# Attention scores for all heads at once on the two row halves, with a new start order, in a fused attention and MLP kernel

## The chip, the cores and the metric

One core of one Trainium2 chip runs the kernel. The metric is the device time in microseconds (us) of one execution. A kernel's time here is the median of four or seven executions; none of them was in the slow state (over 1.5% above the fastest of its kernel). The profile is one execution, whose span (first to last instruction) is about 2 us shorter than its time. In profiles TensorE, which does the matmuls, is PE (its weight loads are PEld), VectorE is DVE, ScalarE is ACT, and GpSimd is POOL, which also issues most of the loads (DMA). TensorE writes its results to PSUM, a memory that the kernel uses in eight banks.

## The reference, cut to what matters

Four batches, 8 heads, 768 positions, head width 64. Each query sees the 96 keys up to itself and the first 8 keys of the batch, with a bias that falls with distance. The result, rearranged to 3072 tokens of 512 numbers, goes through an MLP with a squared relu.

```python
keep = is_global | is_local            # 8 global keys, 96 local keys
scores = scale * q @ k.T + bias        # bias = -slope[h] * dist
a = exp(where(keep, scores, -1e9)); a /= a.sum()
x = (a @ v) rearranged to (3072, 512)
h = x @ w_in                           # 512 x 2048
out = (relu(h) ** 2) @ w_out           # 2048 x 512
```

Work goes by 24 tiles of 128 positions, 6 to a batch. As keys reach back at most 95 positions, a tile needs its own keys and those of the tile before (a batch's first tile only its own). The MLP goes by 12 blocks of two tiles, with w_in and w_out each cut into 8 pieces.

## The kernel before

The program is a list of operations with costs. A small planner in the kernel file orders them when the program is built; that order is then fixed on each engine. `load` names when a late tile's data is expected, and `any_copy` is a copy on either VectorE or ScalarE.

Scores: two heads share the 128 rows. To get the two heads' scores apart with one full-height matmul, q is padded: the rhs holds head 0 over zeros beside zeros over head 1.

```python
for pair in range(0, NPAIR, per):               # one PSUM bank for a head pair
    sc = ps_sc.tile([P, 2, 2, P], FP32)         # 2 banks, used in turn
    for i in range(2):                          # own keys, keys of the tile before
        nc.tensor.matmul(out=sc[:, i, :, :], lhsT=kT[kj][:, p_, :],
                         rhs=qz[zi][:, p_, :, :])    # 256 columns, half of them zeros
    # exp on ScalarE, times exp(bias) on VectorE, then at x v
```

Softmax sums come from a column of ones that stands beside v. It is set first of all:

```python
nc.vector.memset(zero.bitcast(I32), 0)
for j in range(NT):                                    # all 24 tiles
    nc.vector.memset(v_sb[j][:, :, D : D + 1], 1.0)    # the ones columns
make_identity(nc, ident)                               # on POOL
load_qk(1)
# ... masks on POOL ...
load_v(0); load_v(1)
# ... then T2 i0 T3 o0 i1 o1 i2 o2 i3 o3 T4 i4 o4 i5 o5 T5 i6 o6 i7 o7
#     (T: q, k, v of a tile; i, o: a piece of w_in, w_out)
...
ld = plan.op(("load", j), {"POOLQ": 2.6}, emit_load, ..., ready=clock[0])  # tiles 6 to 23
```

The softmax here doesn't subtract the row's maximum and nothing guards it: scores larger than these inputs give would overflow.

## Time and profile before

| | before |
|---|---|
| time | 225.8 us (225.67 to 226.42) |
| TensorE busy | 211.1 us, 94% of a span of 223.7 |
| TensorE's waits from 30 us on | 0.7 us |
| first MLP matmul | 19.38 us |

The lines are in the prediction below. Busy time is the union of records; what an instruction really takes from the next one is read from start to start.

### The profile page before, as it was taken

Reading aid. Unit: us, or ns where it says so; the run is one execution under the profiler, and the core shown is the slowest. Engines: PE = TensorE matmul, PEld = TensorE weight load, DVE = VectorE, ACT = ScalarE, POOL = GpSimd, SP = SyncE. Lnnn points to the kernel's source line nnn. Section 1 sums busy time; section 2 is a strip of 40 time slices with the busy share of each in tenths; the row PEclk is TensorE's granted clock in tenths of the full one; section 3 lists DMA queues with packets and bytes.
Section 4 is the critical chain, followed back from the end, with each engine's and each line's share of the span. In section 5 each row is a group of like instructions: output and inputs, shape, how many; then the busy total and the mean of one; then the engine's idle time right before and its main releaser. Section 6 shows DMA issues by size and latency. Waiting matters only on the chain.

```text
span 223.7 us, 4803 instructions
## 1 busy us (share of the span) xinstructions
PE 211.1 (94%) x1817; PEld 151.9 (68%) x1848; DVE 146.1 (65%) x380; ACT 123.3 (55%) x225; POOL 88.0 (39%) x118
## 2 busy tenths in 40 slices
PE   6499999999999999999999999999999999999992
PEld 2388677765777777766767777776776676676750
DVE  6466857677766868757666866866756856844530
ACT  3359666674755944645644745734645644643530
POOL 8996677799978985505605000000000000000000
PEclk9979999999999999999999999999999999999998
DMA  9999999999999999998999984256524430300202
GB/s 132 102 148 199 183 197 180 175 174 169 167 146 151 152 171 169 134 214 98 163 166 129 124 118 95 67 124 95 143 54 90 131 70 13 117 11 17 94 0 94
DMA packets 115142, 27.83 MB, mean 124 GB/s; under 512 B 105776, under 2 KB 112176, under 8 KB 115120
## 3 DMA queue, kind: packets, MB, share of 16 engines
q0 software_dynamic: 79424, 13.38, 79.5%
q1 hardware_dynamic: 35696, 14.16, 32.6%
q8 instruction: 14, 0.23, 0.4%
q14 instruction: 8, 0.07, 0.1%
HBM read 27.26 MB, written 6.29 MB: 150 GB/s over the span
## 4 chain that ended last, share of the span: by engine, by line
PE 82%; POOL 6%; DVE 4%; DMA 4%; ACT 2%; issue 1%; POOLq 0%
PE acc L723 35%; PE hT L659 35%; PE sc L442 7%; PE po L549 4%; DMA win<-in_moe_w_in_dram 4%; DVE hs L692 2%; POOL v L186 1%; POOL q L186 1%; POOL k L186 1%; ACT hr L680 1%; DVE o L299 1%; POOL win L186 1%; PE trx L611 1%; POOL wout L186 1%; ACT qz L297 1%
## 5 line engine op out<-in xcount | busy, mean ns | idle before, releaser
L659 PE MATMUL hT<-xT,win 128*128 128x256 bf16 x768 | 98.6, 273 | 0.5 <-ACT xT L297 0.4
L680 ACT ACTIVATE hr<-hT 128x512 f32<-128x512 f32 x96 | 57.3, 597 | 74.7 <-PE hT L659 72.7
L723 PE MATMUL acc<-wout,hs 128*128 128x512 bf16 x353 | 94.8, 379 | 1.6
L659 PEld LDWEIGHTS <-win 128*128 128x128 bf16 x768 | 74.7, 98 | 23.4 <-DMA win<-in_moe_w_in_dram 0.7
L692 DVE TENSOR_TENSOR hs<-hr 128x512 bf16<-128x512 f32 x96 | 65.9, 687 | 25.7 <-ACT hr L680 24.3
L723 PEld LDWEIGHTS <-hs 128*128 128x128 bf16 x384 | 34.5, 98 | 22.8
L482 ACT ACTIVATE esc<-sc 128x512 bf16<-128x512 f32 x78 | 46.2, 593 | 2.4 <-PE sc L442 2.3
L442 PE MATMUL sc<-qz,kT 128*128 128x256 bf16 x176 | 35.3, 276 | 0.7 <-ACT at L482 0.4
L503 DVE TENSOR_TENSOR at<-esc,E 128x512 bf16<-128x512 bf16 x78 | 32.4, 417 | 0.1
L186 POOL DMA_DIRECT2D qpad<-in_q_dram x28 | 21.6, 800 | 23.0 <-DMA qz<-qpad 23.0
L186 POOL DMA_DIRECT2D v<-in_v_dram x24 | 22.0, 918 | 2.6 <-DVE E L318 1.7
L186 POOL DMA_DIRECT2D k<-in_k_dram x23 | 21.2, 920 | 3.1 <-PE trx L611 1.8
L575 DVE TENSOR_TENSOR x<-po,rs 128x256 bf16<-128x256 f32 x48 | 20.4, 424 | 1.7
L549 PEld LDWEIGHTS <-at 128*128 128x128 bf16 x352 | 17.2, 99 | 5.9
L574 DVE RECIPROCAL rs<-po 128x4 f32<-128x4 f32 x48 | 8.7, 180 | 18.2 <-PE po L549 17.6
L442 PEld LDWEIGHTS <-kT 128*128 128x128 bf16 x176 | 17.1, 99 | 3.1 <-DVE kT L299 0.8
L549 PE MATMUL po<-v,at 128*128 128x65 bf16 x352 | 18.8, 194 | 0.0
L299 DVE COPY o<-acc 128x512 f32<-128x512 f32 (+1 forms) x12 | 8.0, 664 | 8.2 <-PE acc L723 4.3
L297 ACT COPY o<-acc 128x512 f32<-128x512 f32 (+1 forms) x13 | 7.4, 570 | 5.3 <-PE acc L723 5.2
L297 ACT COPY qz<-trq 64x512 bf16<-64x512 bf16 x10 | 5.8, 580 | 7.5 <-DVE qz L299 5.3
L522 DVE COPY kT<-kT 128x32 bf16<-128x32 bf16 x16 | 3.4, 210 | 9.2 <-PE sc L442 9.2
L186 POOL DMA_DIRECT2D q<-in_q_dram x9 | 8.3, 924 | 1.5 <-DMA wout<-in_moe_w_out_dram 1.2
(52 smaller groups left out, 91.2 us busy)
## 6 DMA issues: line engine op xcount, KB each, us to landing
out_dram<-o SPq DMA_DIRECT2D x23, 256.0 KB, 2.5
v<-in_v_dram POOLq DMA_DIRECT2D x24, 128.0 KB, 6.7
k<-in_k_dram POOLq DMA_DIRECT2D x23, 128.0 KB, 5.7
win<-in_moe_w_in_dram POOLq DMA_DIRECT2D x8, 256.0 KB, 8.4
wout<-in_moe_w_out_dram POOLq DMA_DIRECT2D x8, 256.0 KB, 8.8
qpad<-in_q_dram POOLq DMA_DIRECT2D x28, 64.0 KB, 4.5
q<-in_q_dram POOLq DMA_DIRECT2D x9, 128.0 KB, 7.9
plain_q<-in_q_dram SPq DMA_DIRECT2D x1, 256.0 KB, 3.3
```

Source lines behind the costliest of these rows:

```text
L186: nc.gpsimd.dma_start(out=dst, in_=src)
L297: nc.scalar.copy(dst, src)
L299: nc.vector.tensor_copy(dst, src)
L442: nc.tensor.matmul(out=sc[:, i, :, :], lhsT=kT[kj % NKT][:, p_, :], rhs=qz[zi][:, p_, :, :], start=True, stop=j >= NBIAS, skip_group_check ...
L482: nc.scalar.activation(out=esc, in_=sc.rearrange("p a b c -> p (a b c)"), func=Act.Exp, scale=scale,)
L503: nc.vector.tensor_mul(at, tiles.pop(("esc", j, pair)), bias.rearrange("p a b c -> p (a b c)"))
L549: nc.tensor.matmul(out=po[:, hi, :], lhsT=at[:, pair % 2 if first else i, h % 2, :], rhs=v_sb[kj][:, h, :], start=(i == 0), stop=(i == len ...
L575: nc.vector.tensor_tensor(out=x[:, 4 * hf : 4 * hf + 4, :], in0=po[:, :, :D], in1=rs.to_broadcast([P, 4, D]), op=Alu.mult,)
L659: nc.tensor.matmul(out=hT[:, c, :], lhsT=w_in_sb[s][:, kt, c * P : (c + 1) * P], rhs=tiles["xT", blk][:, kt, :], start=(kt == 0), stop=(kt ...
L680: nc.scalar.activation(hr, tiles.pop(("hT", blk, s)), Act.Relu)
L692: nc.vector.tensor_mul(hs, hr, hr)
L723: nc.tensor.matmul(out=tiles["acc", blk, sub], lhsT=hs[:, c, sub * P : (sub + 1) * P], rhs=w_out_sb[s][:, c, :], start=(s == 0 and c == 0) ...
```

## The change

The intent: halve TensorE's score work by using each half of the rows for one head, free DVE, ACT and DMA of the padding, and shorten the start by building masks on VectorE and loading w_in sooner. The scores of all pairs are made in one block of 16 matmuls into four banks of one ring of six, which also serves the MLP, the transposes and at x v. The diff, cut to its core:

```diff
-    ps_h (3 banks), ps_sc (2), ps_o (1)
+    ps_g = ctx.enter_context(tc.tile_pool(name="ps_g", bufs=NG, space=PSUM))   # 6
-    q_pad, qz (padded, zeroed), kT
+    qkT = [const([P, 2, NPAIR, P], BF16, f"qkT_{i}") for i in range(NKT)]
...
     nc.vector.memset(zero.bitcast(I32), 0)
-    for j in range(NT):
-        nc.vector.memset(v_sb[j][:, :, D : D + 1], 1.0)
-    make_identity(nc, ident)
-    load_qk(1)
+    load_part(0, 1)
     nc.gpsimd.iota(pbi, ...)
-    (cast and two affine_selects on POOL)
+    load_part(1, 1)
     load_v(0)
     load_v(1)
+    for j in range(4):
+        nc.vector.memset(v_sb[j][:, :, D : D + 1], 1.0)
+    (identity and masks by five operations on VectorE)
...
+    for g in range(4, NT, 5):                      # ones columns of tiles 4 to 23
+        o = plan.op(("ones", g), {"DVE": 0.2}, ..., key=4.0 * g - 20, ready=15.0)
+    for w in "i0 T2 i1 T3 i2 o0 i3 o1 i4 o2 T4 i5 o3 i6 o4 T5 i7 o5 o6 o7".split():
...
-                key=base, ready=clock[0],          # late loads: the landing clock
+                key=base, ready=issue[0],          # the issue clock
...
+            for g, pair, at, kt in todo:
+                for odd in range(2):
+                    half = slice(odd * D, (odd + 1) * D)
                     nc.tensor.matmul(
-                        out=sc[:, i, :, :], lhsT=kT[...][:, p_, :], rhs=qz[zi][:, p_, :, :],
+                        out=sc[odd, g][:, at, :],
+                        lhsT=qkT[(j - kt) % NKT][half, 1, pair, :],
+                        rhs=qkT[j % NKT][half, 0, pair, :],
```

The diff also changes how the planner chooses (the weight `URGE`, the engines' starting times), puts an early exponential on ScalarE and joins q and k in one buffer.

## The prediction

> **What bounds the kernel now.** I read the page first (parts 1 and 2), then the waits of TensorE alone, then TensorE's timeline, then the chain and POOL's timeline for the first 30 us.
>
> ```profile
> PE 211.1 (94%) x1817; PEld 151.9 (68%) x1848; DVE 146.1 (65%) x380; ACT 123.3 (55%) x225; POOL 88.0 (39%) x118
> ...
> PE   6499999999999999999999999999999999999992
> ...
> PEclk9979999999999999999999999999999999999998
> ```
>
> The first line gives PE 94% of the span, and the second shows it full in every 5.6 us slice but the first two and the last. The clock is full save in the third slice. (The digits of busy time say "an instruction is under way", not "the array is full"; that needs the next two views.)
>
> The waits of TensorE between 30 and 220 us are two, 0.7 us in all:
>
> ```profile
> PE hT L659 <- ACT xT L297: 0.4, 1, 0.4
> PE sc L442 <- DVE kT L299: 0.3, 1, 0.3
> ```
>
> The timeline of TensorE around 100 us (start, length, what) gives what one instruction really takes from the next, from start to start:
>
> ```profile
> 101.28 1.04 PE L659 MATMUL hT<-xT,win 128*128 128x256 bf16 x8
> ...
> 107.84 0.38 PE L442 MATMUL sc<-qz,kT 128*128 128x256 bf16 x2
> 108.06 1.03 PE L723 MATMUL acc<-wout,hs 128*128 128x512 bf16 x3
> ...
> 110.01 1.04 PE L659 MATMUL hT<-xT,win 128*128 128x256 bf16 x8
> 110.89 0.38 PE L442 MATMUL sc<-qz,kT 128*128 128x256 bf16 x2
> 111.11 1.03 PE L723 MATMUL acc<-wout,hs 128*128 128x512 bf16 x4
> 111.97 0.23 PE L549 MATMUL po<-v,at 128*128 128x65 bf16 x2
> ```
>
> From 110.01 to 110.89, eight matmuls of 256 columns take 0.87 us, 0.109 each (the record says 0.27, which is latency). Two score matmuls take 0.22; four of 512 columns take 0.86, 0.215 each. The same view gives 0.24 for eight of 65 columns (0.030 each) and 0.055 for one of 128 columns. Now I add these up for everything after the step at 30.24 us: 92 steps of the first MLP product x 0.872 = 80.2; about 369 of the second x 0.215 = 79.5; 148 score matmuls x 0.109 = 16.1; 296 of at x v x 0.030 = 9.0; 64 transposes x 0.055 = 3.5. The sum is 188.3 us, and from 30.24 to the end of the last matmul at 219.5 are 189.3 us. So **after 30 us TensorE is full, and only fewer TensorE cycles help there**. Before 30.24 the same adding gives about 17 us of work, so some 13 us are lost: 4.2 until the first q lands, the rest to waits and to a half clock.
>
> The chain and POOL's timeline show what the start hangs on:
>
> ```profile
> 14.96 8.15 DMA win<-in_moe_w_in_dram
> 23.15 1.05 PE hT L659 x8
> ```
>
> ```profile
> 6.87 0.90 POOL L186 DMA_DIRECT2D q<-in_q_dram  x1
> ...
> 9.46 0.81 POOL L186 DMA_DIRECT2D win<-in_moe_w_in_dram  x1
> ...
> 13.49 0.88 POOL L186 DMA_DIRECT2D win<-in_moe_w_in_dram  x1
> 14.27 0.81 POOL L186 DMA_DIRECT2D wout<-in_moe_w_out_dram  x1
> 14.96 0.88 POOL L186 DMA_DIRECT2D win<-in_moe_w_in_dram  x1
> ```
>
> The third w_in piece is issued at 14.96 and lands at 23.1. Before that TensorE waits 2.3 us (8.6 to 10.9) for the q of tile 2, issued only at 6.87, because POOL built the masks until 5.1. The idle stretch is followed by a stretch, 11.5 to 13.9, in which 128-column matmuls come every 0.105 us: the half clock, at a cost of some 1.2 us.
>
> **What the Trainium skill says.** (1) "Perfetto Trace Analysis", its opening note on roofline, calls matmul busy time a bad metric because matmuls are pipelined; the trace agrees (0.27 us recorded, 0.109 us taken), which is why I add start-to-start times. (2) "TensorE: Matmul & The Clock Gate", Part 3, says that matmuls on different row groups run at the same time, a few ns apart, and that a weight load overlaps a matmul only of another row group. The kernel before has no such matmul, so its trace can't tell. (3) "TensorEngine Tiling (Array Packing)", Key Properties: a change of tiling mode drains the engine. Not in this trace either. (4) "PSUM — Partial Sum Buffer", The four PSUM rules: a starting matmul clears the accumulate marks of its whole bank. The new order for tiles 0 to 2 starts four blocks in one bank and only then adds the biases; by that page the first three biases would overwrite their scores. As q and k are 0.1 wide, scaled scores are about 0.01, so I expect about a per cent in some weights, and a pass. It costs no time.
>
> **The change part by part.**
> *Scores.* A tile that isn't the first of its batch had 8 matmuls of 256 columns, half of whose rhs was zero padding: 8 x 0.109 = 0.87 us. It gets 16 of 128 columns on 64 rows. If the two halves run together, that is 8 pairs x 0.055 = 0.44. Going into the mode and out of it costs two drains. I estimate each from the trace as the part of a recorded 128-column matmul (0.22 us) that is not its 0.055, about 0.165, or 0.33 for both, some of it hidden: 0.30. So 0.74, a gain of 0.13 a tile. In the 17 such tiles after tile 3 that is 2.2 us. The three later first tiles go from 0.44 to 0.22 + 0.30 = 0.52 and lose 0.24 together. Tiles 1 to 3 are split in two groups, 2 x 0.52 = 1.04, and lose 0.5 together, in a stretch that isn't full. **Net: -1.9 us in the full stretch.** I was free to choose the drain; at 0.25 for both the gain is 0.9 us more.
>
> *q unpadded, one transpose.* For tiles 0 to 9, two half copies of q (0.42 on DVE, 0.58 on ACT) become one; the four clears of qz (0.48 each) go. From tile 10 on, 28 padded q loads become 14, and two DMA transposes of 4.3 and 4.2 us to landing become one. POOL's 23.0 us wait for the padded buffers goes too. None of it lies on the path: TensorE waits 0.7 us in 190. **0 us**, but the DMA engines are freer.
>
> *Masks on DVE.* POOL loses the identity (0.5 us) and the cast and two selects (1.3 us), so everything it issues comes 0.7 to 1.8 us sooner, q of tile 2 at 5.6 in place of 6.9 even with a w_in piece ahead of it. DVE gains three small operations on 256 columns, some 0.3 to 0.4 each, where it idled (0.94 us before pb).
>
> *w_in first.* Between 5.7 and 26 us the loads land at about 0.9 us for a q, k or v tile and 1.4 for a weight piece (k, v of tile 3 and four weight pieces land between 15.9 and 23.15: 8 tile units in 7.3 us). Taking 5.0 us for the first landing and these paces, I get: v1 at 7.7, w_in 0 at 9.1, tile 2 by 11.8, w_in 1 at 13.2, tile 3 by 15.9, w_in 2 at 17.3 (before: 23.1), w_out 0 at 18.7, w_in 3 at 20 (26), w_in 4 at 23 (about 30). The first MLP step then waits for tiles 0 and 1 and not for weights, and starts near 15 us in place of 19.4; six steps can be done by 22 where before there were two. The lost time by 30 us would be the 4.2 at the start, about 3 of waiting and slow clock, and about 2 where w_out or tile 5 (now after w_in 6 and w_out 4, about 35 us) comes late: 9 to 9.5 in place of 13. **-3.8 us.**
>
> *One ring of six banks.* Two score banks, three for the MLP and one for at x v become six for all. A tile's scores take four at once and ACT needs 4 x 0.59 = 2.4 us to drain them, in which two banks are left for the MLP. TensorE can fill that with the second product. **+0.3 us** for places where the planned order doesn't fit.
>
> Sum: -1.9 - 3.8 + 0.3 = -5.4 us; 225.9 - 5.4 = **220.5 us**.
>
> **The rivals.**
> A: *the halves don't overlap.* 16 x 0.055 + 0.30 = 1.18 against 0.87, a loss of 0.31 x 17 = 5.3 us in the full stretch in place of a gain of 1.9: 225.9 + 5.3 - 3.8 + 0.3 = 228. For it: nothing in this trace shows overlap. Against it: the second page above, and that weight loads clearly keep up with matmuls every 0.030 us at at x v.
> B: *the ring becomes the bound.* Four score banks wait for ACT, which also has relus in its queue; if TensorE loses 0.3 us a tile in 20 tiles, that is 6 us and the time is near 226. For it: the two-bank rest, and a ring freed in order. Against it: ACT is busy 55% and DVE 65%, and PE has 14 buffers of squared activations to work from.
> C: *the start is bound by DMA anyway.* The digits of DMA are 9 in the first 20 slices; bringing w_in forward delays w_out and tile 5. Then the lost time falls only from 13 to 12: 223. For it: the same bytes must land by 40 us. Against it: TensorE is already full at 30 in the old order.
> D: *both gains come in full*: lost time 8 us, drains 0.25: 217.5.
>
> **Range and chances.** A has perhaps 5%, B in a strong form 7%, C 25%, my sum or better the rest. The 2% line is 221.4, only 0.9 us above my figure, so the chance of faster by over 2% is 0.58, of the same 0.37, of slower 0.05. The range is 216.5 to 225.
>
> **What would show it.** In the changed profile: the score block of 16 matmuls takes about 0.74 us from the last matmul before it to the first after it, with pairs of starts close together (right) or 0.9 us and more of even steps (A). TensorE's waits after 30 us stay below 2 us (right), or show hT or sc waiting for exp on ACT (B). The first MLP step starts near 15 us, and the third doesn't wait for w_in; if TensorE is idle for w_out or for tile 4 or 5 between 24 and 40 us, it is C. The lost time, span less the sum of start-to-start work, falls by about 4 us. I am wrong if the full stretch gets longer.

## The result, and the profile after

| | before | after |
|---|---|---|
| time, us | 225.81 (225.67 to 226.42) | **241.17** (240.67 to 241.57) |
| span of the profiled run, us | 223.7 | 239.8 |
| first MLP matmul, us | 19.38 | 23.36 |

The changed kernel is 6.7% slower: ratio 1.067, interval 1.065 to 1.070. A ratio here is the mean time of one kernel's runs over that of the other's in the same rounds, so it is not quite the ratio of the medians quoted. Where kernels of two submissions are compared, I take the difference of their ratios, in per cent of the 226 us.

The page after (busy shares, tenths of busy time in 40 slices of 6 us, granted clock):

```profile
PE 210.0 (88%) x1992; PEld 145.6 (61%) x2024; DVE 142.6 (59%) x372; ACT 122.4 (51%) x224; POOL 73.8 (31%) x91
...
PE   5189302999999999999999999999999999999983
...
DVE  0235004878746866867568677675676776764530
...
PEclk9999955899999999999999999999999999999998
```

TensorE's second slice (6 to 12 us) and its fifth to seventh (24 to 42) are mostly empty, and the clock falls to about half in the second gap and just behind it. VectorE, which never idled like this before, is empty in the first, the fifth and the sixth slice. After slice eight all looks as before. TensorE's waits from 30 us to the last matmul are these three, one of them huge:

```profile
PE sc L428 <- DVE qkT L302: 14.6, 1, 14.6
PE acc L716 <- DVE hs L685: 0.6, 1, 0.6
PE trx L604 <- DVE x L569: 0.4, 1, 0.4
```

TensorE waits for a copy on VectorE. What VectorE itself does is in its timeline (start, length, what; in brackets the idle time before it and who ended it). In the kernel before, the ones columns are set at once (nineteen in this row, five in another):

```profile
1.11 0.70 DVE L243 MEMSET v<- 128x8 bf16 x19
```

In the changed kernel:

```profile
0.86 0.27 DVE L235 MEMSET zero<- 128x256 int32 x1 [0.86 <-PEq L791]
7.97 0.07 DVE L249 MEMSET v<- 128x8 bf16 x1 [6.83 <-DMA v<-in_v_dram]
10.64 0.21 DVE L250 TENSOR_SCALAR ident<-pbi 128x128 f32<-128x128 int32 x1 [2.60 <-issue]
...
22.45 0.42 DVE L302 COPY xT<-trx 128x512 bf16<-128x512 bf16 x1 [0.53 <-PE trx L604]
31.37 0.07 DVE L275 MEMSET v<- 128x8 bf16 x1 [8.49 <-DMA v<-in_v_dram]
39.15 0.07 DVE L275 MEMSET v<- 128x8 bf16 x1 [7.71 <-DMA v<-in_v_dram]
```

These are the ones columns. Each takes 0.07 us, but each now waits for the load of v into the other columns of the same buffer, since the load was issued first. VectorE does nothing else meanwhile, though TensorE's transposes for its copies at 39.22 and 40.10 us were done by 24.9: everything behind the memsets stands. First these are identity, masks and the copies of tile 0 (until 10.6 us; the profile calls the second wait, 2.60 us, "issue", but v of tile 1 lands at 10.57), then all of VectorE's work from 22.9 to 39.15 us, when v of tile 5 lands. The planner did not know: its operation `("ones", g)` names no load that it depends on. The memsets and the load write different elements (columns 64 and 0 to 63 of each head), so no value depends on their order; the program that was built orders them all the same. The two stops in TensorE's timeline:

```profile
10.91 1.97 PE L370 MATMUL tr<-ident,plain 128*128 128x128 f32 x8 [6.12 <-DVE ident L250]
...
25.57 0.41 PE L541 MATMUL po<-v,at 128*128 128x65 bf16 x8
40.57 0.29 PE L428 MATMUL sc<-qkT 64*128 64x128 bf16 x2 [14.60 <-DVE qkT L302]
```

The chain that ended last names the same thing, a load on the path where before there was TensorE:

```profile
30.64 8.42 DMA v<-in_v_dram
39.76 0.42 DVE x L569
40.19 0.34 DVE qkT L302
40.57 0.61 PE sc L428 x7
```

POOL is caught too: the load of v of tile 2 waits until its memset has run, and all later loads with it (the profile names a VectorE operation that runs beside the memsets).

```profile
6.87 0.93 POOL L189 DMA_DIRECT2D qk<-in_k_dram  x1
11.05 0.96 POOL L189 DMA_DIRECT2D v<-in_v_dram  x1 [3.25 <-DVE ident L251]
```

And the part that the change was made for works better than I forecast. A score block in TensorE's timeline:

```profile
101.64 1.03 PE L716 MATMUL acc<-wout,hs 128*128 128x512 bf16 x4
102.60 0.23 PE L428 MATMUL sc<-qkT 64*128 64x128 bf16 x2
102.67 0.22 PE L428 MATMUL sc<-qkT,qkT 64*128 64x128 bf16 x2
...
103.00 0.22 PE L428 MATMUL sc<-qkT,qkT 64*128 64x128 bf16 x2
103.15 1.05 PE L652 MATMUL hT<-xT,win 128*128 128x256 bf16 x8
```

Two matmuls start every 0.056 us. The four of 512 columns should be done 0.86 us after 101.64, at 102.50; the next MLP matmul starts at 103.15. So the block costs 0.65 us in place of 8 x 0.109 = 0.87. (Some expectations below count from the block's first start, 102.60, and so say 0.55.)

### The profile page after: what moved, and what is told of

It is laid out like the page before. It is cut to its first block, busy times and chain, and to the rows that moved or that the text cites. A ratio compares the mean times of both kernels' runs of the same rounds, so it can differ in the third digit from the quotient of the medians.

```text
span 239.8 us, 5051 instructions
## 1 busy us (share of the span) xinstructions
PE 210.0 (88%) x1992; PEld 145.6 (61%) x2024; DVE 142.6 (59%) x372; ACT 122.4 (51%) x224; POOL 73.8 (31%) x91
## 4 chain that ended last, share of the span: by engine, by line
PE 78%; DMA 9%; POOL 5%; DVE 3%; issue 3%; ACT 1%; POOLq 0%
PE hT L652 35%; PE acc L716 33%; DMA v<-in_v_dram 5%; PE sc L428 4%; DMA wout<-in_moe_w_out_dram 4%; PE po L541 4%; POOL qk L189 2%; DVE hs L685 1%; POOL win L189 1%; PE tr L370 1%; PE trx L604 1%; POOL v L189 1%; POOL wout L189 1%; DVE x L569 1%; DVE at L499 0%
## 5 line engine op out<-in xcount | busy, mean ns | idle before, releaser
L716 PE MATMUL acc<-wout,hs 128*128 128x512 bf16 x352 | 91.6, 380 | 2.0 <-DVE hs L685 0.6
L652 PEld LDWEIGHTS <-win 128*128 128x128 bf16 x768 | 71.3, 98 | 17.3 <-issue 0.2
L474 ACT ACTIVATE esc<-sc 128x512 bf16<-128x512 f32 x78 | 42.4, 599 | 29.5 <-PE sc L428 29.5
L716 PEld LDWEIGHTS <-hs 128*128 128x128 bf16 x384 | 36.7, 98 | 29.1 <-DVE hs L685 1.2
L189 POOL DMA_DIRECT2D qk<-in_q_dram x23 | 21.1, 915 | 26.9 <-DMA qkT<-qk 17.4
L428 PE MATMUL sc<-qkT 64*128 64x128 bf16 x192 | 13.9, 228 | 15.6 <-DVE qkT L302 15.3
L428 PEld LDWEIGHTS <-qkT 64*128 64x128 bf16 x352 | 10.4, 97 | 24.9 <-DVE qkT L302 15.8
L189 POOL DMA_DIRECT2D qk<-in_k_dram x23 | 21.0, 914 | 0.1
L428 PE MATMUL sc<-qkT,qkT 64*128 64x128 bf16 x160 | 12.0, 223 | 0.0
L474 ACT ACTIVATE at<-sc 128x512 bf16<-128x512 f32 x10 | 5.4, 594 | 4.4 <-PE sc L438 4.3
```

The source lines that it names most:

```text
L189: nc.gpsimd.dma_start(out=dst, in_=src)
L428: nc.tensor.matmul(out=sc[odd, g][:, at, :], lhsT=qkT[(j - kt) % NKT][half, 1, pair, :], rhs=qkT[j % NKT][half, 0, pair, :], start=True, s ...
L474: nc.scalar.activation(out=esc, in_=tiles.pop(("sc", j, odd, g)).rearrange("p a c -> p (a c)"), func=Act.Exp, scale=scale,)
L652: nc.tensor.matmul(out=hT[:, c, :], lhsT=w_in_sb[s][:, kt, c * P : (c + 1) * P], rhs=tiles["xT", blk][:, kt, :], start=(kt == 0), stop=(kt ...
L716: nc.tensor.matmul(out=tiles["acc", blk, sub], lhsT=hs[:, c, sub * P : (sub + 1) * P], rhs=w_out_sb[s][:, c, :], start=(s == 0 and c == 0) ...
```

## The experiments

In all of them the file is the changed kernel unless it says otherwise. The theories: **M**, the memsets behind the loads; **O** and **R**, the load order or the ring starve TensorE.

**1. All ones columns first (e1).**

```diff
     nc.vector.memset(zero.bitcast(I32), 0)
+    for j in range(NT):
+        nc.vector.memset(v_sb[j][:, :, D : D + 1], 1.0)
     load_part(0, 1)
-    (the memsets of tiles 0 to 3 after load_v(1), and the planned groups of 4 to 23)
```

> The changed kernel with one thing put back: the ones columns of all 24 v tiles are set before the first v load is issued, as in the kernel before. Theory M (the memsets of the ones columns stand behind the v loads in VectorE's strict order, and stop it twice, until 10.8 and until 39.2 us): both stops go, TensorE is full from about 25 to 30 us on, and the time is about 215 us (work 199 + lost 9.5 + the 6.4 between the last matmul and the reported time). Rival O (the new load order, w_out and tile 5 late, starves the start): the time stays near 238 to 241. Rival R (the ring of six banks and the four-bank score block stall TensorE): waits of TensorE stay, above 230.

Measured: 221.95 us (ratio 0.982, 0.980 to 0.984), 19 us less than the changed kernel. VectorE now sets all ones columns at once, and of TensorE's waits from 30 us on only small ones are left, so M holds and O and R fall:

```profile
1.11 0.88 DVE L237 MEMSET v<- 128x8 bf16 x24
```

```profile
PE tr L363 <- DMA qk<-in_q_dram: 1.0, 1, 1.0
PE acc L709 <- DVE hs L678: 0.6, 1, 0.6
PE acc L709 <- DMA wout<-in_moe_w_out_dram: 0.4, 1, 0.4
```

But 215 was too low by 7 us. It took over the prediction's lost time of 9.5 us, which was too small; 1.4 us of the 7 come up in experiment 5, and the rest was not taken apart.

**2. Only the first four first (e3), only the later twenty first (e4).** Each undoes one of the two stops.

> The changed kernel with only the first four ones columns set before the loads; the later groups stay where the plan puts them. Theory M: the first stop (to 10.8 us) goes, the second stays and ends when v of tile 5 lands, some 4 us sooner than 39.2 as POOL no longer waits: about 236 to 237. Rivals O and R: no change, 240 to 241.

> The changed kernel with only the later 20 ones columns set at the start, the first four left behind the loads of v. Theory M: the first stop stays (transposes of tile 0 at 10.9 us), the second goes: about 4 to 6 us above the kernel with both mended, 219 to 221. Rivals O and R: 240 to 241.

Measured: 239.19 (1.060) and 224.42 us (0.993). Against e1 the second stop alone costs 7.8%, 17.6 us, and the first alone 1.1%, 2.4 us. The first stop holds VectorE until 9.4 us in e4, and it costs only half of the 5.1 us by which TensorE's first transposes come late (9.64 us against 4.58), because what follows there waits for loads anyway: e1's TensorE waits 3.7 us for loads in all, and the waits of e4 show none. The two together, 20.0 us, agree with the 8.5% (19.3 us) between e1 and the changed kernel.

**3. The kernel before with its memsets late (e2).**

```diff
-    for j in range(NT):
-        nc.vector.memset(v_sb[j][:, :, D : D + 1], 1.0)
     make_identity(nc, ident)
...
     load_v(0)
     load_v(1)
+    for j in range(NT):
+        nc.vector.memset(v_sb[j][:, :, D : D + 1], 1.0)
```

> The kernel before with nothing changed but that its 24 ones columns are set after the loads of v of tiles 0 and 1 are issued. Theory M: VectorE stops until v of tile 1 lands, near 10 us, and POOL waits with v of tile 2: 3 to 5 us slower, 229 to 231. If the order of a memset and a load were harmless (rivals O and R): 226.

Measured: 232.26 us (1.029, 1.025 to 1.031). The same move does harm without anything else of the change: 6.4 us, somewhat more than I expected and more than the 2.4 us of the first stop in e4. Here the profile names v for both waits, and TensorE's first transposes come at 11.70 us in place of 4.21:

```profile
8.82 0.07 DVE L259 MEMSET v<- 128x8 bf16 x1 [7.69 <-DMA v<-in_v_dram]
10.35 0.67 DVE L259 MEMSET v<- 128x8 bf16 x18 [1.46 <-DMA v<-in_v_dram]
```

**4. Is the start paced by bytes or by their order? (e5, e7, e8, all on e1.)** e5 takes the old load order, e7 puts tiles 2 to 5 further to the front, e8 builds identity and masks on POOL again.

> The mended kernel (all ones columns first, 221.95 us) with the load order of the kernel before. Theory W (w_in first shortens the start, as the prediction said, by 3 to 4 us): 225 to 226. Theory D (the start is paced by the bytes that must land, and the order of the pieces moves the idle time about but hardly its sum): 221 to 223, with the first MLP step later than 16.5 us all the same.

> The mended kernel with tiles 2 to 5 one place further to the front of the loads (tile 2 before the first w_in, tile 5 after four w_in and two w_out in place of seven and five). Theory D (bytes pace the start): within 1 us of 221.95. Theory W or any theory in which an order is worth several us: at least 2 us off, either way; faster if TensorE lacked tiles (it waited for q of tiles 3 and 6), slower if it lacked weights.

> The mended kernel with identity and masks built on POOL again, as before. If taking them off POOL brings the loads forward and that counts: 1 to 1.5 us slower, 223 to 223.5, as POOL's issues come 1.3 to 1.8 us later. Theory D: the DMA engines have enough queued from 6 us on, so that it counts only while the first loads fill them: 0 to 1 us, 222 to 223.

Measured: e5 225.13 us (0.995), e7 221.98 (0.983), e8 227.08 (1.007). Read by themselves, these numbers say that w_in first is worth 3 us and masks on VectorE 5, against e7, where another order changes nothing. The sum is also too much: e1 gains 4 us in all. TensorE's timeline of e8 shows another cause:

```profile
44.01 0.61 PE L364 MATMUL tr<-ident,qk 128*128 128x128 bf16 x4 [3.63 <-DMA qk<-in_q_dram]
```

TensorE stands for 3.6 us for q of tile 6 (in e5 2.6 us, in e1 0.95, at 42.0 us), and the four matmuls of 512 columns that follow in e8 take 1.71 us in place of 0.86. In the kernel before the same transposes stand much later in TensorE's order:

```profile
49.23 0.39 PE L375 MATMUL trq<-ident,q 128*128 128x128 bf16 x4
```

The planner of the changed kernel takes a late tile's load to be ready by the time at which POOL has *issued* the loads before it (`issue[0]`), while the kernel before took the time at which they have *landed*. In e1 that q is issued at 33.3 us and lands at 41.9: the order was made for data that was not there yet.

**5. The landing clock back (e9 on e1, e10 on e8, e11 on e5).**

```diff
-                key=base, ready=issue[0],
+                key=base, ready=issue[1] - 2.0,
```

> The mended kernel (221.95 us) with one number of the planning put right: loads of tile 6 and later become ready by the landing clock, as in the kernel before, in place of the issue clock, so that the fixed order of TensorE places the transposes of tile 6 later (before: at 49 us; mended kernel: at 42.0, after a wait of 0.95 us for its q). Theory P (the order is planned for a q of tile 6 that has not come): that wait goes, and the time falls by 0.5 to 1.5 us, to 220.5 to 221.5. Theory D alone (bytes pace the start): no change.

> The kernel with masks on POOL (227.1 us) with the same number put right. It waited 3.6 us for q of tile 6 at 44 us and then ran at half clock. Theory P: most of its loss of 5.1 us was this wait, so 222 to 223.5, at most 2 us above the kernel with masks on VectorE and the same number. If masks on POOL cost 5 us by themselves: 226 or more.

> The kernel with the old load order (225.1 us) with the same number put right. It waited 2.6 us for q of tile 6. Theory P: 221.5 to 222.5, so that w_in first is worth 1 us or less. Theory W (w_in first is worth 3 us by itself): 224 or more.

Measured: e9 **220.65** us (0.976, 0.973 to 0.979), e10 221.51 (0.980), e11 220.90 (0.977). In e9 these transposes come at 45.2 us and wait for nothing:

```profile
45.20 0.61 PE L363 MATMUL tr<-ident,qk 128*128 128x128 bf16 x8
```

So the issue clock cost 0.6% (1.4 us) in e1, 1.8% (4.1) in e5 and 2.7% (6.0) in e8. With it put right, masks on VectorE are worth 0.4% (0.9 us) and w_in first 0.1% (0.2 us); the intervals of e9, e10 and e11 overlap, so neither is clear of noise. What experiment 4 seemed to show of these two was nearly all one planning error, met at different times. So the order of the loads hardly counts; that bytes pace the start is not shown by this. e9 beats both kernels.

**6. What makes the score block short (e6 on e1, e12 on e9).** e6 sorts the block's matmuls, all even heads first and then all odd ones. e12 puts all of them on the upper half; its scores are wrong on purpose. It passed the comparison with the reference all the same, which shows how little the scores weigh in this result.

```diff
 e6
-            for g, pair, at, kt in todo:
-                for odd in range(2):
+            for odd in range(2):
+                for g, pair, at, kt in todo:
 e12
-                    half = slice(odd * D, (odd + 1) * D)
+                    half = slice(0, D)
```

> The mended kernel with the score block's matmuls sorted, all of the even heads (upper rows) first and then all of the odd ones, so that neighbours are on the same half of the rows and can't run side by side. Theory S (the block takes 0.55 us because neighbours on different halves overlap): the block grows from 0.55 to 0.9 us or more, at 0.055 a matmul or above, and the time by at least 17 x 0.35 + 3 x 0.17 = 6.5 us, to 228 or more. Rival (128-column matmuls on 64 rows are just quicker by themselves): the block stays near 0.55 and the time near 222.

> Wrong results on purpose: the kernel with the number put right, with all score matmuls on the upper half of the rows (the odd heads read the even heads' q and k), so that no two can run side by side in any order. Theory S (overlap of the halves makes the block short): the block grows from 0.55 us to about 16 x 0.055 + 0.11 = 1.0 us, and the time by 17 x 0.45 + 3 x 0.22 = 8 us. Rival (half-height matmuls are quick by themselves): no change.

Measured: e6 225.25 us (0.998), e12 228.38 (1.011). The block of e12:

```profile
107.47 1.03 PE L709 MATMUL acc<-wout,hs 128*128 128x512 bf16 x4
108.43 0.28 PE L421 MATMUL sc<-qkT 64*128 64x128 bf16 x2
108.55 0.27 PE L421 MATMUL sc<-qkT,qkT 64*128 64x128 bf16 x2
...
109.43 1.05 PE L645 MATMUL hT<-xT,win 128*128 128x256 bf16 x8
```

Two matmuls now take 0.11 us, twice as long, and the block 109.43 - (107.47 + 0.86) = 1.10 us. A first tile's block of 8 grows from 0.43 to 0.65. 17 x 0.45 + 3 x 0.22 = 8.3 us were to be expected from that, and 3.4%, 7.8 us, were measured. So half-height matmuls are no quicker by themselves; the overlap is what makes the block short. e6 was a surprise:

```profile
107.57 0.22 PE L421 MATMUL sc<-qkT,qkT 64*128 64x128 bf16 x1
107.63 0.23 PE L421 MATMUL sc<-qkT 64*128 64x128 bf16 x2
...
107.79 0.24 PE L421 MATMUL sc<-qkT,qkT 64*128 64x128 bf16 x2
107.87 0.22 PE L421 MATMUL sc<-qkT 64*128 64x128 bf16 x1
...
108.19 1.05 PE L645 MATMUL hT<-xT,win 128*128 128x256 bf16 x8
```

The records show four single starts, then four double ones, then four single ones. Eight even matmuls stand before eight odd ones in the program, so four odd ones must have run beside the last four even ones, ahead of their turn. A first tile's block, four even and then four odd, runs in four pairs and takes 0.44 us, no longer than in e9. The block of 16 takes 0.90 us (the 512-column matmuls before it start at 106.43 and should be done at 107.29), between 0.65 and 1.10, and the time lies between as well. My 228 assumed no overlap at all in e6.

## Why the prediction was wrong

I forecast 220.5 us and a range of 216.5 to 225; it was 241.2, outside it, and with the wrong sign.

- **The bound.** "After 30 us TensorE is full, and only fewer TensorE cycles help there": right for the kernel before, and for e9 (0.6 us of waits). In the changed kernel TensorE stands until 40.57 us and is full only after that.
- **The step that failed: the list of parts.** The prediction's parts "Masks on DVE" and "w_in first" give VectorE "three small operations ... where it idled" and the first MLP step "near 15 us". They leave out a move that stands in the diff: the memsets of the ones columns went from before the loads of v to behind them. Its cost is not in the sum and not among rivals A to D. It is 19.3 us (e1 against the changed kernel), 2.4 from the first stop and 17.6 from the second. The first MLP step came at 23.36 us.
- **Scores, -1.9 us in the full stretch.** Mechanism right, size off: pairs start together (as the Trainium skill's "TensorE: Matmul & The Clock Gate", Part 3, has it; here 2 to 3 ns apart), and two 128-column matmuls take 0.056 us. The term that was mis-sized is the drain: I took 0.30 us for both, and the block of 0.65 us less 8 x 0.055 leaves 0.21. The gain is then, by this count, 17 x (0.87 - 0.65) = 3.7 us, and a first tile's block of 8 breaks even (0.43 against 0.44). Rival A was tested by force in e12, and its 1.18 us were close to the 1.10 measured.
- **Start, -3.8 us.** Mis-sized even with the memsets mended. Against before, e9 gains 2.4%, 5.4 us; less 3.7 for the scores, 1.7 us are left for everything else in the change. Masks on VectorE are about 0.9 of these and w_in first 0.2. The first MLP step of e9 does come at 15.95 us, about as forecast, but four steps and not six have begun by 22 us, and then TensorE waits for w_in, w_out and q of tile 4 (0.3, 0.2 and 1.0 us). By the prediction's own sign that is rival C; whether bytes set these times is not shown. Rival D's 217.5 does not follow from its own terms either: 225.9 - 5 - 2.8 = 218.1.
- **The ring, +0.3 us.** Harmless: in e9 TensorE waits 0.6 us in all between 30 and 220 us. Rival B falls.
- **A reading.** The trace before could tell half of the skill's claim (2): its 256-column matmuls on all rows follow each other at 0.109 us, each with its own weight load, so these loads were hidden without another row group.
- **What I did not see either** is the planner's clock for late loads, 1.4 us in e1. It is one word in the diff.
- **A right number for the wrong reason.** e9, with both slips mended, stands at 220.65 us, next to my 220.5. That is no credit to the sum: its score term was too small and its start term too large by about the same 2 us.
- **The biases of tiles 0 to 2.** The kernel passes, as expected, but so does e12 with the wrong scores in half of the heads. A pass shows nothing here, and whether scores were overwritten stays open.

## What to carry to other kernels

When a diff moves a cheap instruction, ask what it now stands behind, not what it costs: twenty-four memsets of 0.07 us cost 19 us because they were put behind loads, and all other work of VectorE stood behind them. Read every line of a diff as a possible wait, those included that belong to no headline. And before crediting a part with what its removal costs, look where the loss shows up in the trace: two parts here seemed worth 3 and 5 us, and were worth about 0.2 and 0.9, neither clear of noise, once one wrong ready time was mended.

## What the Trainium skill lacked or had wrong

- "TensorE: Matmul & The Clock Gate", Part 3, says that matmuls keep program order in start and end. In e6 four matmuls of the lower half started beside the last four of the upper half, ahead of their place: 12 start times about 0.06 us apart for 16 matmuls.
- The same page, "Back-to-back issue gap", gives about 81 ns for 128 columns and 131 ns for 512 as the sustained pace with weight loads. Here it was 55 ns and 215 ns, each matmul with its own weight load; what the section gives for a single matmul, about 56 and 216 ns, fits. Nor did a load need another row group to be hidden, as Part 3 says (Part 2 does allow other cases): sixteen half-height matmuls on one row group took 0.055 us each (e12).
- "TensorEngine Tiling (Array Packing)", Key Properties, says that a change of tiling mode drains the engine, and gives no size. Into the row mode and out again was 0.21 us together (0.65 less 8 x 0.055; a first tile's block, 0.43 less 4 x 0.055, and e12's, 1.10 less 16 x 0.055, leave the same to 0.01), if all of it is the drain.
- No page that I used says that a memset and a load into different columns of one buffer are put in order: 6.8, 8.5 and 7.7 us of wait for memsets of 0.07 us. By which rule they are taken to overlap was not tested.
